# V in five blocks and tokens gathered from the output: one change to an attention kernel with routed experts

## The chip, the cores and the metric

The kernel runs on one core of a Trainium2 chip. The metric is device time in microseconds: the median of several executions of the whole program.

## The reference

There are two stages. The first is attention over 8 batches, 8 heads, 576 tokens and 64 channels. A query keeps only the keys whose score lies within `tau` of its best one:

```python
scores = q @ k.transpose(0, 1, 3, 2) / np.sqrt(64)
scores = np.where(scores >= scores.max(-1, keepdims=True) - tau, scores, -1e9)
attn = np.exp(scores - scores.max(-1, keepdims=True))
x = (attn / (attn.sum(-1, keepdims=True) + 1e-9)) @ v      # then laid out as 4608 tokens x 512
```

The second sends tokens through one of eight experts each. A token takes part if `x @ w_skip > 0`; the other tokens are the output as they stand:

```python
out = x.copy()
e_idx = np.argmax(xc @ w_gate, axis=1)                     # xc: the tokens that take part
out[token] = x[token] + gate_w[token] * (np.maximum(x[token] @ w1[e], 0) @ w2[e])
```

All is float32; the kernel keeps this accuracy by splitting each factor of a product into a high and a low part and adding three products.

## The kernel before

**Attention** is done head pair by head pair, 32 of them, four for each batch. For a pair `g`, `plan_pair` loads q and k (`raw`), ACT or DVE casts them to a high part and POOL or DVE subtracts to get the low part, both in a staging buffer `hl` (one of four buffers of the ring `wr`). `plan_dist` then spreads them by six transfers into the tile `QK`, and `plan_blk` by two into `BD` (the 64 last tokens of both heads). A staging buffer is free again when those transfers have read it. `plan_score` makes row maxima (PE, then DVE), `plan_thresh` and `plan_trow` turn them into a threshold row that ACT copies into QK (L848), `plan_weights` makes scores again, transposed, with the threshold subtracted (PE), `e` by an exponential (ACT, L884) and `p` by masking (DVE, L889). Two blocks of `p` share one of `PFB` buffers. From it come a half-precision high part (`phh`, ACT or DVE) and the rest (`phl`, POOL, L926); when POOL is done with it the buffer is free. `plan_av` multiplies both with V (PE, L954 to L958), and ACT copies the result out. POOL then normalises it: `fx` (L1006) into the batch's rows `xb`, `ft` (L1019) into `x2`, which holds the last 64 tokens of two batches.

A head has 576 = 4 x 128 + 64 keys. V is laid out on the host in `NT` = 6 blocks of 128 rows for each head: four full ones, one with the last 64 keys in rows 0 to 63, and one with the same keys in rows 64 to 127. The tail block of p holds the tail keys of the even head in its upper half and of the odd head in its lower half, so an even head uses block 4 and an odd one block 5. `plan_v` loads V of a batch in four transfers, finds a power of two to scale it (ACT, L623, with a sum of magnitudes), scales it (L686), casts it to half precision (L689) and subtracts (POOL, L692).

Finished rows of a batch are stored twice by `plan_rows` and `plan_tails`: to `xs`, a DRAM copy that tokens are gathered from, and to `out`. `plan_logits` and `plan_gate` compute the gate; records (token, weight) are scattered on POOL's queue into the list `lst` (L1312), sorted by expert.

**The order** of all this work on each engine isn't the program's. Every step is an `Op` with a duration for each engine that may do it, a key, and its predecessors; rings of buffers (`take`, `free`) add predecessors. `Plan.place` simulates the engines and a single DMA link with booked transfer times (`pl.dma(..., xfer)`), and puts the steps in the order in which they come free. `Plan.run` repeats this with priorities disturbed by each number in `SEEDS`, the last pass emitting the instructions. The order so found is fixed at build time, and each engine runs its own part in order.

**The experts** follow in program order. `plan_early` and the last part of the plan do layer 1 of a first job, 256 tokens of the fullest expert; then eight jobs follow. For each, `gather_x` turns the list's token numbers into indices and gathers rows into `xg` on POOL's queue. A list entry without a token holds 65536. `prep_x` transposes and splits, `layer1` and `layer2` multiply, `split_w` splits the weights (ACT, then DVE and POOL by turns, L1734), and `store` adds and scatters to `out`. Tokens beyond the planned capacity would be done by a loop at the end, whose blocks `late_table` finds in small operations on one partition, one after each block of layer 1.

Of the kernel before, what the change touches and what calls it, by code (L numbers as in the profile page):

```python
# [27 lines left out]
H = 8  # L28
# [25 lines left out]
NT = NM + 2  # L54
# [6 lines left out]
PFB = 3  # L61
# [233 lines left out]
def attn_moe_kernel(ctx: ExitStack, tc: tile.TileContext, qk, vl, tau, wg, w1, w2, out):  # L295
# [14 lines left out]
    xs = dp.tile([NTOK, DM], F32, name="xs")  # L310
# [78 lines left out]
    linit = cp.tile([P, NB, 2], F32, name="linit")  # L389
# [82 lines left out]
    def init():  # L472
# [17 lines left out]
    def plan_pair(g):  # L490
# [16 lines left out]
        ld = pl.dma(k - OFF["ld"], load, (ring.take("xb", 2) if g == 1 else ring.take("raw", 1)) + ([(T["neg"],)] if g else []), [1.8], 0.46)  # L507
# [40 lines left out]
    def plan_blk(g):  # L548
# [12 lines left out]
        T["bd", g] = pl.dma(k - OFF["bd"] if g else -200, blk, [*T["lo", g]] + ring.take("BD", 2), [0.41, 0.41], 0.66)  # L561
        T["hld", g] += [T["bd", g]]

    def plan_dist(g, h):
# [10 lines left out]
        for i in range(3):  # L575
# [11 lines left out]
            mine.append(pl.dma(kd + 0.1 * i, dist, [*c] + ([(mine[0],)] if mine else qr), [1.5], 0.65))  # L587
# [3 lines left out]
    def plan_v(b):  # L591
# [16 lines left out]
        for i in range(4):  # L608
# [5 lines left out]
                    [1.15],  # L614
# [245 lines left out]
    def plan_weights(g, i):  # L860
# [75 lines left out]
        elif i == STEP - 1:  # L936
            plan_av(g, 1, [(i - 2, [0, 1]), (NM, [NM + 1]), (i, [2, 3])], n)

    def plan_av(g, h, parts, n):
# [23 lines left out]
        for j, (i, kts) in enumerate(parts):  # L963
# [9 lines left out]
            if NM not in kts:  # L973
                ring.free("ph", [x]) if NM + 1 not in kts else ring.free("tp", [x])
# [364 lines left out]
    kk = cp.tile([P, 2, E, E], F32, name="kk")  # L1339
# [3 lines left out]
    idg = cp.tile([P, E, CT], I32, name="idg")  # L1343
    evs = {}

    class Job:
        def __init__(self, cap, rec, ids, idg):
            self.cap, self.rec, self.ids, self.idg = cap, rec, ids, idg
# [5 lines left out]
    j0 = Job(CAPE, rec0, id0[:, 0, :], id0[:, 1, :])  # L1354
    jobs = [j0] + [
        Job(CAPS[e] - (CAPE if e == 0 else 0), recs[:, e], ids[:, e], idg[:, e]) for e in range(E)
# [34 lines left out]
    def plan_early(k, j):  # L1391
# [24 lines left out]
        def ids():  # L1416
            nc.vector.tensor_copy(id0[:, 0, :], rec0[:, :, 0])
            nc.vector.tensor_scalar(id0[:, 1, :], rec0[:, :, 0], float(NTOK - S - 1), None, op0=ALU.min)
# [5 lines left out]
        for t in range(CAPE // P):  # L1424

            def ga(t=t):
                if t == 0:
                    early["xg"] = cp.tile([P, CAPE // P, DM], F32, name="xg0")
                gather(early["xg"][:, t, :], id0[:, 1, t : t + 1], NTOK - S)
# [232 lines left out]
    T["init"] = pl.dma(OFF["init"], init, [settle[1]], [0.1, 0.3, 1.2, 0.4])  # L1662
# [53 lines left out]
    tab = cp.tile([1, 2 * NOV + 1], I32, name="tab")  # L1716
    NK = E + 1
    rows = []
# [60 lines left out]
    def store(j, t, yp):  # L1779
# [11 lines left out]
        for x in rows:  # L1791
# [46 lines left out]
    def late_table():  # L1838
# [4 lines left out]
        ce = late.tile([1, 8, NK], F32, name="ce")  # L1843
        capv, capb, nbk, cum, prv, colb, eve, tmp = (ce[:, i, :] for i in range(8))
# [32 lines left out]
        yield  # L1877
        nc.vector.tensor_scalar(
# [21 lines left out]
        yield  # L1900
        lp_ = [1, NOV, NK]
# [12 lines left out]
        ej = late.tile([1, 2, NOV], F32, name="ej")  # L1914
        for i, src in enumerate((eve, colb)):
# [8 lines left out]
        nc.vector.tensor_copy(tab[:, 0 : 2 * NOV], ej.rearrange("p a j -> p (a j)"))  # L1924
# [6 lines left out]
    for part in parts:  # L1931
        part()
    w1s = early["w1"]
# [48 lines left out]
    with tc.For_i(0, nit, 1) as it:  # L1982
# [15 lines left out]
        nc.sync.dma_start(wb, w2v[ds(ev, 1)].rearrange("a p t f -> p (a t) f"))  # L1998
# [82 lines left out]
```

## Time and profile before

| what | value |
|---|---|
| median of 3 runs | 942.32 us (941.84 to 942.96) |
| profiled execution | 938.75 us |
| span of its trace, first to last instruction | 937.0 us |
| mean granted TensorE clock | 0.966 |
| busy share of the span | PE 93%, DVE 74%, ACT 67%, POOL 71% |
| transfers | 157.37 MB, mean 168 GB/s |

The trace is of one execution. "Busy" is the share of the time in which an engine executes; an engine waits in order for the inputs of its next instruction, and the trace names what ended the wait. The clock is the share of full speed that the chip granted to TensorE, which has two levels, 1.2 and 2.4 GHz. A DMA share of 1 means that all sixteen DMA engines move data all the time.

### The profile page before, as it was taken

How to read it: one execution, taken by the hardware profiler on the slowest of the kernel's cores; microseconds unless marked ns; L12 is line 12 of the kernel's file. 1: busy time of each engine (PE TensorE's matmuls, PEld its weight loads, DVE VectorE, ACT ScalarE, POOL GpSimd, SP SyncE). 2: the span in 40 equal slices, each digit the busy share in tenths (PEclk: the TensorE clock that was granted, in tenths of full speed). 3: DMA queues.
4: the chain of work that ended last, by engine and by line, in shares of the span. 5: the costliest groups of instructions: out<-in, count | busy, mean ns of one | idle time of the engine just before them, and what ended most of it. 6: DMA issues, size and time to landing. Idle time of an engine off the chain costs nothing. (4 is left out here: it accounts for less than half of the span.)

```text
span 937.0 us, 24810 instructions
## 1 busy us (share of the span) xinstructions
PE 870.6 (93%) x9630; PEld 808.6 (86%) x9630; DVE 691.5 (74%) x1622; ACT 628.7 (67%) x947; POOL 662.2 (71%) x452
## 2 busy tenths in 40 slices
PE   6899998998999999999998999978889999999994
PEld 3789997997999998899997898867879898999993
DVE  4888986888888888889895898967525554487770
ACT  1588986886998897899896699768414442455450
POOL 5288884896788898999987799968334545365451
PEclk8799998999999999999997999989989999999998
DMA  7987676669679759877866674623356535544530
GB/s 207 217 224 174 130 202 178 146 164 267 135 156 265 171 110 259 188 160 200 224 147 184 173 168 91 176 91 114 113 162 228 193 102 181 180 144 180 178 115 18
DMA packets 81790, 157.37 MB, mean 168 GB/s; under 512 B 28619, under 2 KB 28875, under 8 KB 81672
## 3 DMA queue, kind: packets, MB, share of 16 engines
q1 hardware_dynamic: 76984, 145.49, 59.4%
q0 software_dynamic: 4544, 10.28, 3.3%
q8 instruction: 77, 1.26, 0.5%
q14 instruction: 41, 0.34, 0.1%
q10 hardware_dynamic: 144, 0.00, 0.0%
HBM read 70.78 MB, written 24.78 MB: 102 GB/s over the span
## 5 line engine op out<-in xcount | busy, mean ns | idle before, releaser
L926 POOL TENSOR_TENSOR phl<-p,phh 128x1152 f16<-128x1152 f32 x128 | 305.4, 2394 | 58.5 <-ACT phh L465 16.1
L748 DVE TENSOR_REDUCE mx<-shp 128x1 f32<-128x288 f32 x558 | 236.7, 448 | 48.7 <-PE shp L743 45.5
L884 ACT ACTIVATE e<-sps,ntau 128x576 f32<-128x576 f32 x288 | 211.0, 740 | 57.4 <-PE sps L716 54.3
L889 DVE SCALAR_TENSOR_TENSOR p<-sps,e 128x576 f32<-128x576 f32 x288 | 215.4, 751 | 33.1 <-ACT e L884 24.9
L743 PE MATMUL shp<-QK 128*128 128x288 f32 x992 | 201.6, 314 | 6.1 <-DVE mx L748 3.2
L716 PE MATMUL sps<-QK 128*128 128x288 f32 x1024 | 191.7, 312 | 10.7 <-ACT QK L848 5.4
L716 PEld LDWEIGHTS sps<-QK 128*128 128x128 f32 x1024 | 148.7, 193 | 19.2 <-ACT QK L848 7.1
L743 PEld LDWEIGHTS shp<-QK 128*128 128x128 f32 x992 | 149.7, 191 | 12.8 <-DVE mx L748 7.8
L465 ACT ACTIVATE phh<-p 128x1152 f16<-128x1152 f32 x117 | 136.4, 1166 | 12.2 <-DVE p L889 8.1
L958 PE MATMUL avp<-Vh,phl 128*128 128x65 f16 x1280 | 130.8, 194 | 7.4 <-POOL phl L926 7.3
L954 PE MATMUL avp<-Vh,phh 128*128 128x65 f16 x1280 | 132.8, 196 | 2.6 <-ACT a L465 2.5
L957 PE MATMUL avp<-Vl,phh 128*128 128x64 f16 x1280 | 131.6, 193 | 0.0
L958 PEld LDWEIGHTS <-phl 128*128 128x128 f16 x1280 | 118.0, 98 | 8.2 <-POOL phl L926 8.1
L954 PEld LDWEIGHTS <-phh 128*128 128x128 f16 x1280 | 116.8, 98 | 8.1
L957 PEld LDWEIGHTS <-phh 128*128 128x128 f16 x1280 | 118.1, 99 | 3.0 <-issue 3.0
L1734 POOL TENSOR_TENSOR wl<-wr,wh 128x1024 fp32r<-128x1024 f32 x28 | 72.5, 2601 | 35.4 <-ACT wh L1733 30.0
L1771 PE MATMUL hps<-xh,wl 128*128 128x256 f32 (+4 forms) x256 | 77.1, 301 | 0.0
L1771 PE MATMUL hps<-xh,wh 128*128 128x256 f32 (+4 forms) x248 | 76.5, 308 | 0.1
L1771 PE MATMUL hps<-xl,wh 128*128 128x256 f32 (+4 forms) x248 | 75.0, 303 | 0.0
L1772 ACT ACTIVATE QK<-hps 128x256 fp32r<-128x256 f32 (+4 forms) x64 | 26.9, 421 | 68.9 <-PE hps L1771 68.2
L1783 POOL DMA_INDIRECT out<-o,ids x21 | 21.0, 1001 | 71.5 <-DVE o L1782 30.0
L692 POOL TENSOR_TENSOR Vl<-vraw,Vh 128x768 f16<-128x768 f32 x32 | 51.0, 1600 | 22.3 <-ACT Vh L689 22.1
(261 smaller groups left out, 1912.1 us busy)
## 6 DMA issues: line engine op xcount, KB each, us to landing
QK<-hl SPq DMA_DIRECT2D x192, 288.0 KB
wr<-in_w SPq DMA_DIRECT2D x31, 1024.0 KB
raw<-in_qk SPq DMA_DIRECT2D x32, 576.0 KB
vraw<-in_vl SPq DMA_DIRECT2D x32, 384.0 KB
xs<-xb SPq DMA_DIRECT2D x32, 256.0 KB
out<-xb SPq DMA_DIRECT2D x32, 256.0 KB
BD<-hl SPq DMA_DIRECT2D x64, 64.0 KB
xs<-x SPq DMA_DIRECT2D x8, 128.0 KB
```

Of the source, the lines that this page charges most:

```text
L465: nc.scalar.activation(dst, src, AF.Copy)
L716: nc.tensor.matmul(ps[:, j, 0:HS], w_, x_[:, js], start=(i == 0), stop=(i == len(mm) - 1))
L743: nc.tensor.matmul(ps[:, 0:HS], w_, x_[:, js], start=(q == 0), stop=(q == len(mm) - 1))
L748: nc.vector.tensor_reduce(T["mx", g][:, o, j : j + 1], T.pop(("S", g, i, j))[:, 0:HS], AX.X, ALU.max)
L884: nc.scalar.activation(e, T["W", g, i][:, :, 0:HS], AF.Exp, bias=ntau, scale=0.125)
L889: nc.vector.scalar_tensor_tensor(T[z][:, kt % 2].rearrange("p (a b) -> p a b", a=2), T.pop(("W", g, i))[:, :, 0:HS], 0.0, T.pop(("e", g, i ...
L926: nc.gpsimd.tensor_tensor(T["pl", g, i], T.pop(z)[:, 0:nk], T["ph", g, i], op=ALU.subtract)
L954: nc.tensor.matmul(pv[:, c, :], x, Vh[:, vh, kt, :], start=(j + q + c == 0), stop=False, skip_group_check=True)
L957: nc.tensor.matmul(pv[:, c, 0:D], x, Vl[:, vh, kt, :], start=False, stop=False, skip_group_check=True)
L958: nc.tensor.matmul(pv[:, c, :], y, Vh[:, vh, kt, :], start=False, stop=(c == NM), skip_group_check=True)
L1734: lo[q % 2].tensor_tensor(w[1][:, sl], rs, w[0][:, sl].bitcast(F32), op=ALU.subtract)
L1771: nc.tensor.matmul(hp_[:, 0:cap], w_, x, start=(i == 0), stop=(i == len(mm) - 1))
```

## The change

V loses its sixth block: block 4 holds the tail keys of even heads in its upper half and of odd heads in its lower half, and all heads use it. The copy `xs` goes, with its stores and an initialising write; gathers read `out`, and list entries without a token, whose numbers lie beyond the bound, are left out by the gather instead of being clipped, so the two `xg` buffers are zeroed once ahead. The gathers and scatters of different experts are declared independent. The late loop, which may no longer read a row that it has written, gets a count of valid entries. `linit` shares the memory of `kk`. There is a fourth p buffer, the planner's durations for most transfers are longer, and the order comes from other seeds.

```diff
-NT = NM + 2
+NT = NM + 1
-PFB = 3
+PFB = 4
...
 SEEDS = (
-    1000005, 1000007, 1000359, 1000371, ...
+    1000005, 1000007, 1000025, 1001369, ...
...
-    xs = dp.tile([NTOK, DM], F32, name="xs")
...
-            nc.vector.memset(vt[:, :, NM:, D : D + 1], 0.0)
-            nc.vector.memset(vt[0:TL, :, NM, D : D + 1], 1.0)
-            nc.vector.memset(vt[TL:P, :, NM + 1, D : D + 1], 1.0)
+            nc.vector.memset(vt[:, :, NM, D : D + 1], 0.0)
+            nc.vector.memset(vt[0:TL, 0::2, NM, D : D + 1], 1.0)
+            nc.vector.memset(vt[TL:P, 1::2, NM, D : D + 1], 1.0)
...
     def gather(dst, idx, n):
-        nc.gpsimd.indirect_dma_start(
+        return nc.gpsimd.indirect_dma_start(
             dst,
             None,
-            xs[0:n, :],
+            out[0:n, :],
...
-        nc.sync.dma_start(
-            xs[NTOK - S - TL : NTOK - S, :].rearrange("p (o c) -> p o c", c=P),
-            ident[0:TL].rearrange("p (o c) -> p o c", o=1).broadcast_to([TL, DM // P, P]),
-        )
...
-        ld = pl.dma(k - OFF["ld"], load, ..., [1.8], 0.46)
+        ld = pl.dma(k - OFF["ld"], load, ..., [2.0], 0.46)
-        T["bd", g] = pl.dma(..., [0.41, 0.41], 0.66)
+        T["bd", g] = pl.dma(..., [0.46, 0.46], 0.66)
-            mine.append(pl.dma(kd + 0.1 * i, dist, ..., [1.5], 0.65))
+            mine.append(pl.dma(kd + 0.1 * i, dist, ..., [1.6], 0.65))
-                    [1.15],
+                    [1.1],
...
-            plan_av(g, 1, [(i - 2, [0, 1]), (NM, [NM + 1]), (i, [2, 3])], n)
+            plan_av(g, 1, [(i - 2, [0, 1]), (NM, [NM]), (i, [2, 3])], n)
...
         for t in range(NM):
-            for i, dst in enumerate((xs, out)):
-
-                def st(t=t, dst=dst):
-                    r0 = b * S + t * P
-                    nc.sync.dma_start(dst[r0 : r0 + P, :], T["x", b][:, t, :])
-
-                rd.append(pl.dma(k + OFF["row"] + OFF["rsp"] * (2 * t + i), st, T["xm", b, HP - 1], [0.69], 0.7))
+            def st(t=t):
+                r0 = b * S + t * P
+                nc.sync.dma_start(out[r0 : r0 + P, :], T["x", b][:, t, :])
+
+            rd.append(pl.dma(k + OFF["row"] + OFF["rsp"] * 2 * t, st, T["xm", b, HP - 1], [0.75], 0.7))
...
-                for dst in (xs, out):
-                    nc.sync.dma_start(dst[r0 : r0 + TL, :], T["x2"][i * TL : (i + 1) * TL, :])
-        s = pl.dma(k + 1, st, xtm, [0.4] * 4)
+                nc.sync.dma_start(out[r0 : r0 + TL, :], T["x2"][i * TL : (i + 1) * TL, :])
+        s = pl.dma(k + 1, st, xtm, [0.45] * 2)
...
     def gather_x(j):
         nc.vector.tensor_copy(j.ids[:, 0 : j.nb], j.rec[:, 0 : j.nb, 0])
-        nc.vector.tensor_scalar(j.idg[:, 0 : j.nb], j.rec[:, 0 : j.nb, 0], float(NTOK - 1), None, op0=ALU.min)
-        j.xg = mp.tile([P, CT, DM], F32, name="xg", tag="xg")
+        j.xg = xgs.pop(0) if xgs else mp.tile([P, CT, DM], F32, name="xg", tag="xg")
         for t in range(j.nb):
             m = j.m(t)
-            gather(j.xg[0:m, t, :], j.idg[0:m, t : t + 1], NTOK)
+            gt = gather(j.xg[0:m, t, :], j.ids[0:m, t : t + 1], NTOK)
+            for x in rows:
+                tc.declare_no_dep(gt.ins, x.ins, reason="it uses no row of another expert")
+            reads.append(gt)
...
-        for x in rows:
+        for x in rows + reads:
             tc.declare_no_dep(sc.ins, x.ins, reason="every token goes to one expert")
...
+        nc.vector.tensor_copy(capv[:, E:NK], nbk[:, E:NK])
+        nc.vector.tensor_tensor(fin, prv, capb, op=ALU.subtract)
+        nc.vector.scalar_tensor_tensor(fin, fin, float(P), capv, op0=ALU.mult, op1=ALU.add)
-        for i, src in enumerate((eve, colb)):
+        for i, src in enumerate((eve, colb, fin)):
...
+        nc.vector.tensor_tensor(done, ej[:, 2, :], thr, op=ALU.subtract)
...
+    xgs = [mp.tile([P, CT, DM], F32, name="xg", tag="xg") for _ in range(2)]
+    for x in xgs:
+        nc.vector.memset(x, 0.0)
     w1s = early["w1"]
     gather_x(jobs[1])
...
+        dn = lp.tile([1, 1], F32, name="dn")
+        nc.sync.dma_start(dn, done[0:1, ds(it, 1)])
+        nc.tensor.matmul(dp_[:, 0:1], onesr, dn, start=True, stop=True)
+        nc.vector.tensor_scalar(dm, dp_[:, 0:1], iop, SENT, op0=ALU.is_gt, op1=ALU.mult)
+        nc.vector.tensor_tensor(li[:, 0:1], rc[:, 0:1], dm, op=ALU.add)
...
-    vl = np.zeros((B, P, H, NM + 2, D), np.float32)
+    vl = np.zeros((B, P, H, NM + 1, D), np.float32)
-    vl[:, 0:TL, :, NM] = vt
-    vl[:, TL:, :, NM + 1] = vt
+    vl[:, 0:TL, 0::2, NM] = vt[:, :, 0::2]
+    vl[:, TL:, 1::2, NM] = vt[:, :, 1::2]
```

## Rows read from the trace of the kernel before

**Rows 1.** Stretches: PE, PEld, DVE, ACT, POOL busy (instructions); clock, DMA share, GB/s.

```profile
40.00:640.00 600.00, 567.81 (x7583) 535.89 (x7582) 507.47 (x1292) 496.45 (x734) 502.36 (x310) 0.98 0.71 175
...
700.00:900.00 200.00, 198.03 (x1264) 184.10 (x1263) 123.05 (x174) 86.66 (x143) 105.20 (x62) 1.00 0.52 176
...
128.00:136.00 8.00, 7.90 (x118) 7.54 (x116) 7.00 (x14) 7.18 (x11) 6.88 (x5) 1.00 1.01 281
...
140.00:160.00 20.00, 16.26 (x167) 15.44 (x165) 12.82 (x27) 12.21 (x18) 7.53 (x6) 0.83 0.79 208
500.00:520.00 20.00, 15.49 (x98) 14.85 (x96) 8.90 (x24) 8.08 (x13) 10.58 (x9) 0.66 0.70 196
10.00:40.00 30.00, 21.14 (x91) 15.34 (x89) 16.54 (x53) 10.91 (x16) 7.89 (x35) 0.72 1.05 240
```

**Rows 2.** The instructions of line 842, one for each head pair.

```profile
L842 PE MATMUL sps<-ident,nh x32: 270/272/276, 37.8 to 629.6; 128*2 128x128 f32 x32
```

**Rows 3.** Waits of PE, 40 to 640 us: total, times, longest.

```profile
PE avp L958 <- POOL phl L926: 7.3, 5, 5.3
PE sps L716 <- ACT QK L848: 5.4, 4, 3.7
PE gps L1062 <- POOL x L1019: 3.6, 1, 3.6
...
PE avp L954 <- ACT a L465: 2.2, 3, 1.1
```

**Rows 4.** Timeline of SyncE's DMA issues, 128 to 140 us: start, length.

```profile
129.71 3.07 SPq L1125 DMA_DIRECT2D out<-xb  x3
132.83 2.95 SPq L1125 DMA_DIRECT2D xs<-xb  x3
...
139.38 2.30 SPq L581 DMA_DIRECT2D QK<-hl  x1
```

**Rows 5.** Timeline, 138 to 153 us; in brackets the idle time before.

```profile
143.16 1.16 ACT L465 ACTIVATE hl<-raw 128x1152 fp32r<-128x1152 f32 x1 [6.29 <-DMA QK<-hl]
...
145.44 0.81 PE L716 MATMUL sps<-QK 128*128 128x288 f32 x4 [3.74 <-ACT QK L848]
```

**Rows 6.** Timeline, 498 to 514 us, POOL.

```profile
505.35 0.39 POOL L1019 TENSOR_TENSOR x<-a,z 64x128 f32<-64x128 f32 x1 [3.63 <-DMA lst<-rec,si]
```

**Rows 7.** Timeline, 617 to 640 us, DVE.

```profile
623.80 0.76 DVE L889 SCALAR_TENSOR_TENSOR p<-sps,e 128x576 f32<-128x576 f32 x1 [3.85 <-POOL phl L926]
```

**Rows 8.** DMA issues: count, size of one, or us to landing.

```profile
vraw<-in_vl SPq DMA_DIRECT2D x32, 384.0 KB
xs<-xb SPq DMA_DIRECT2D x32, 256.0 KB
...
lst<-rec,si POOLq DMA_INDIRECT x36, 3.9
```

**Rows 9.** Groups by line and shape: busy us, mean ns, idle before.

```profile
L692 POOL TENSOR_TENSOR Vl<-vraw,Vh 128x768 f16<-128x768 f32 x32 | 51.0, 1600 | 22.3 <-ACT Vh L689 22.1
...
L686 ACT ACTIVATE vraw<-vraw,vmx 128x768 f32<-128x768 f32 x32 | 29.6, 939 | 0.0
...
L689 ACT ACTIVATE Vh<-vraw 128x768 f16<-128x768 f32 x32 | 26.9, 854 | 0.0
...
L623 ACT ACTIVATE Vh<-vraw 128x1536 f16<-128x1536 f32 x16 | 23.7, 1484 | 16.5 <-DMA vraw<-in_vl 16.5
```

**Rows 10.** The same view of DVE in the first 20 us.

```profile
L359 DVE MEMSET QK<- 64x1152 f32 x2 | 2.0, 1018 | 0.4 <-issue 0.4
```

**Rows 11.** Timelines of POOL, DVE and PE, 640 to 715 us.

```profile
676.77 1.94 POOL L1312 DMA_INDIRECT lst<-rec,si  x1 [0.30 <-DVE wl L1734]
679.01 0.97 POOL L1312 DMA_INDIRECT lst<-rec,si  x1 [0.30 <-issue]
...
684.13 0.17 DVE L1739 CAST ids<-recs 128x2 int32<-128x2 f32 x1 [5.13 <-DMA recs<-lst]
...
688.54 0.33 PE L1753 MATMUL xtp<-ident,xg 128*128 128x128 f32 x1 [2.22 <-DMA xg<-xs,idg]
```

More of the change, by code (lines that the diff above doesn't have):

```diff
@@ L82 @@
 SEEDS = (
[5 rows of a table removed]
+    1000005, 1000007, 1000025, 1001369, 1001397, 1001554, 1001677, 1001694, 1001761, 1001833, 1002643, 1002698,
+    1002871, 1003002, 1003249, 1003775, 1003868, 1006562,
 )
@@ L505, in gate_q @@
             nc.vector.tensor_scalar(q, q, tpos, None, op0=ALU.mult)
-        ld = pl.dma(k - OFF["ld"], load, (ring.take("xb", 2) if g == 1 else ring.take("raw", 1)) + ([(T["neg"],)] if g else []), [1.8], 0.46)
+        ld = pl.dma(k - OFF["ld"], load, (ring.take("xb", 2) if g == 1 else ring.take("raw", 1)) + ([(T["neg"],)] if g else []), [2.0], 0.46)
         x = ld if g else pl.op(k - OFF["hl"], gate_q, [ld], {DVE: 0.37})
@@ L559, in blk @@
                 )
-        T["bd", g] = pl.dma(k - OFF["bd"] if g else -200, blk, [*T["lo", g]] + ring.take("BD", 2), [0.41, 0.41], 0.66)
+        T["bd", g] = pl.dma(k - OFF["bd"] if g else -200, blk, [*T["lo", g]] + ring.take("BD", 2), [0.46, 0.46], 0.66)
         T["hld", g] += [T["bd", g]]
@@ L585, in dist @@
                     nc.sync.dma_start(dst[D:P, RQ2 : RK3 + 1], src[:, HQH : HKL + 1 : 3])
-            mine.append(pl.dma(kd + 0.1 * i, dist, [*c] + ([(mine[0],)] if mine else qr), [1.5], 0.65))
+            mine.append(pl.dma(kd + 0.1 * i, dist, [*c] + ([(mine[0],)] if mine else qr), [1.6], 0.65))
         T["qk", g, h] = mine
@@ L973, in plan_av @@
             if NM not in kts:
-                ring.free("ph", [x]) if NM + 1 not in kts else ring.free("tp", [x])
+                ring.free("ph", [x])
+            elif h:
+                ring.free("tp", [x])
         def cpy(e):
@@ L1338, in attn_moe_kernel @@
     tabp = cp.tile([1, E], I32, name="tabp")
-    kk = cp.tile([P, 2, E, E], F32, name="kk")
     k0, oh = kk[:, 0], kk[:, 1]
@@ L1342, in attn_moe_kernel, with __init__ @@
     ids = cp.tile([P, E, CT], I32, name="ids")
-    idg = cp.tile([P, E, CT], I32, name="idg")
     evs = {}
     class Job:
-        def __init__(self, cap, rec, ids, idg):
-            self.cap, self.rec, self.ids, self.idg = cap, rec, ids, idg
+        def __init__(self, cap, rec, ids):
+            self.cap, self.rec, self.ids = cap, rec, ids
             self.nb = -(-cap // P)
@@ L1352, in m @@
             return min(P, self.cap - t * P)
-    j0 = Job(CAPE, rec0, id0[:, 0, :], id0[:, 1, :])
+    j0 = Job(CAPE, rec0, id0[:, 0, :])
     jobs = [j0] + [
-        Job(CAPS[e] - (CAPE if e == 0 else 0), recs[:, e], ids[:, e], idg[:, e]) for e in range(E)
+        Job(CAPS[e] - (CAPE if e == 0 else 0), recs[:, e], ids[:, e]) for e in range(E)
     ]
@@ L1417, in ids @@
             nc.vector.tensor_copy(id0[:, 0, :], rec0[:, :, 0])
-            nc.vector.tensor_scalar(id0[:, 1, :], rec0[:, :, 0], float(NTOK - S - 1), None, op0=ALU.min)
+            nc.vector.tensor_scalar(id0[:, 1, :], rec0[:, :, 0], float(NTOK - S - TL - 1), None, op0=ALU.min)
         o = pl.op(k + 1, ids, [o], {DVE: 0.15})
@@ L1428, in ga @@
                     early["xg"] = cp.tile([P, CAPE // P, DM], F32, name="xg0")
-                gather(early["xg"][:, t, :], id0[:, 1, t : t + 1], NTOK - S)
+                gather(early["xg"][:, t, :], id0[:, 1, t : t + 1], NTOK - S - TL)
             gs.append(pl.op(k + 2, ga, [o, *stored] + [(y,) for y in gs[-1:]], {POOL: 1.04}, lat=3.0, port=()))
@@ L1661, in attn_moe_kernel @@
     T["settle"] = settle
-    T["init"] = pl.dma(OFF["init"], init, [settle[1]], [0.1, 0.3, 1.2, 0.4])
+    T["init"] = pl.dma(OFF["init"], init, [settle[1]], [0.1, 0.3, 1.2])
     T["start"][1] = [(T["qk", 0, 1][-1],)]
@@ L1716, in attn_moe_kernel @@
     tab = cp.tile([1, 2 * NOV + 1], I32, name="tab")
+    done = cp.tile([1, NOV], F32, name="done")
     NK = E + 1
-    rows = []
+    rows, reads = [], []
     def split_w(src, raws=(), lo=(nc.vector, nc.gpsimd)):
@@ L1842, in late_table @@
         yield
-        ce = late.tile([1, 8, NK], F32, name="ce")
-        capv, capb, nbk, cum, prv, colb, eve, tmp = (ce[:, i, :] for i in range(8))
+        ce = late.tile([1, 9, NK], F32, name="ce")
+        capv, capb, nbk, cum, prv, colb, eve, tmp, fin = (ce[:, i, :] for i in range(9))
         kc = kk[r0, 0]
@@ L1877, in late_table @@
         yield
+        nc.vector.tensor_copy(capv[:, E:NK], nbk[:, E:NK])
+        yield
         nc.vector.tensor_scalar(
@@ L1900, in late_table @@
         yield
+        nc.vector.tensor_tensor(fin, prv, capb, op=ALU.subtract)
+        yield
+        nc.vector.scalar_tensor_tensor(fin, fin, float(P), capv, op0=ALU.mult, op1=ALU.add)
+        yield
         lp_ = [1, NOV, NK]
@@ L1913, in late_table @@
         yield
-        ej = late.tile([1, 2, NOV], F32, name="ej")
-        for i, src in enumerate((eve, colb)):
+        ej = late.tile([1, 3, NOV], F32, name="ej")
+        for i, src in enumerate((eve, colb, fin)):
             nc.vector.tensor_tensor(cm[:, 1], cm[:, 0], rowb(src), op=ALU.mult)
@@ L1923, in late_table @@
         yield
-        nc.vector.tensor_copy(tab[:, 0 : 2 * NOV], ej.rearrange("p a j -> p (a j)"))
+        nc.vector.tensor_tensor(done, ej[:, 2, :], thr, op=ALU.subtract)
+        yield
+        nc.vector.tensor_copy(tab[:, 0 : 2 * NOV], ej[:, 0:2].rearrange("p a j -> p (a j)"))
         yield
@@ L2003, in attn_moe_kernel @@
         nc.gpsimd.indirect_dma_start(
-            xo, None, xs[:, :], bass.IndirectOffsetOnAxis(ap=li[:, 1:2], axis=0), bounds_check=NTOK - 1, oob_is_err=False
+            xo, None, out[:, :], bass.IndirectOffsetOnAxis(ap=li[:, 1:2], axis=0), bounds_check=NTOK - 1, oob_is_err=False
         )
@@ L2055, in layout @@
         "in_qk": qk,
-        "in_vl": vl.reshape(B, P, H * (NM + 2) * D),
+        "in_vl": vl.reshape(B, P, H * (NM + 1) * D),
         "in_tau": np.asarray(tau, np.float32).reshape(1),
```

6 lines of the change are left out of this document (4 added, 2 removed), and 5 rows, old and new, of the table SEEDS.

## The prediction

> **What bounds the kernel now.** I read the stretches first. From 40 to 640 us the kernel does attention: TensorE (PE) is busy 567.81 of 600 us, VectorE (DVE), ScalarE (ACT) and GpSimd (POOL) 507, 496 and 502 each [rows 1]. From 700 to 900 us it does the experts, with PE busy 198.03 of 200. So the experts give back 2 us at most, and nearly all that this change can move is the 32.2 us that PE idles in attention, and what the lower level of its clock costs there: the clock is 0.98 on the mean, 2% of 600, some 12 us. Nothing else fills 900 us as closely, so I price every edit by what it does to PE's waits.
>
> A head pair passes every (629.6 - 37.8) / 31 = 19.1 us [rows 2]. The waits of PE in attention [rows 3] show who ends them: the low half of p by POOL 7.3 us, of which one wait alone is 5.3; the threshold copy by ACT 5.4, one alone 3.7; a normalised tail by POOL 3.6, a single wait; the copy of an attention result by ACT 2.2. The idle time is thus partly three large stalls (5.3, 3.7 and 3.6, 12.6 of 32.2 us) and partly crumbs.
>
> Stall A, at 140 us. SyncE issues three row stores to `out` from 129.71 and three to `xs` from 132.83 and, behind them, the loads that spread a pair into QK, the last at 139.38 [rows 4]. In 128 to 136 us the DMA engines are full (share 1.01, 281 GB/s) [rows 1]. ACT's cast of the next pair needs its staging buffer back from those spreading transfers and waits 6.29 us for them; ACT takes its work in order, so the threshold copies behind it are late, and PE waits 3.74 us at 145.44 [rows 5]. After it PE runs at 0.83 of its clock through 140 to 160 us, a third of that time at the lower level (1.2 GHz): 20 x 0.17 = 3.4 us. The stall costs about 7.1 us.
>
> Stall B, at 505 us. POOL's product x (L1019) waits 3.63 us until the list scatters issued just before it have landed, and PE's transpose of it waits as long [rows 3, 6]. In 500 to 520 us the clock is 0.66 [rows 1], so 20 x 0.34 = 6.8 us more are lost: 10.4 us.
>
> Stall C, at 620 us, is POOL late with a low half (the 5.3 us of [rows 3]); meanwhile DVE's next p waits 3.85 us, because all three p buffers wait for POOL [rows 7].
>
> **The change, part by part.** *No second copy.* Of 64 row stores of 256 KB the 32 to `xs` go [rows 8], with half of the sixteen tail stores and one initialising store. For one batch that is 4 x 0.262 = 1.05 MB; at the 281 GB/s of the full stretch, 3.7 us of transfer in front of the spreading loads. ACT's wait of 6.29 becomes 2.6, and PE's 3.74 next to nothing: 3.7 saved. What is late next is ACT's own backlog, which DVE's and PE's queued work covers. With a gap that short the clock may hold; I take half of its 3.4 us. Together 5.4 us; from below 0 (the new order can put other transfers there), from above the whole 7.1. At the other batch ends I take nothing: PE's table of waits names no other one of size that a transfer ends. SyncE issues 41 stores fewer; it is on no wait of PE.
>
> The gathers read `out` instead of `xs`: equal rows, equal size, and the same stores have to land before them. Scatters to `out` of other experts are declared independent, so no wait is added.
>
> *V in five blocks.* V loads shrink from 384 KB by a sixth [rows 8]; the ACT passes over V from 1536 and 768 elements to 1280 and 640, POOL's from 768 to 640 [rows 9]. From 1484 and 854 ns an element of ACT costs (1484 - 854) / 768 = 0.82 ns: 16 x 256 x 0.82 = 3.4 us for the first pass and 32 x 128 x 0.82 = 3.4 us for each of the other two, 10.1 us in all; in plain proportion it is (16 x 1484 + 32 x (939 + 854)) / 6 = 13.5. POOL saves up to 32 x 1600 / 6 = 8.5 us beside it. Neither engine sets the pace by itself. Outside the three stalls, PE's large waits on ACT and POOL are 2.0 + 1.7 + 2.2 = 5.9 of its 32.2 us idle [rows 3], 18%, so I count 18% of 10.1, 1.9 us. The rest is covered by PE's and DVE's own work. The ends are 0 and 13.5. PE's products with V stay equal in number and size, since each head used only one of the two tail blocks.
>
> At the start, 10 to 40 us, the DMA engines are full too (1.05, 240 GB/s) [rows 1], and 0.26 MB of V less is 1.1 us; part of V comes behind the first spreading loads, so I take 0.6. The ends are 0 and 1.1.
>
> *Fourth p buffer.* Nothing in it makes POOL faster. In stall C PE itself waits for POOL, so the 3.85 us of DVE are mostly hidden behind that; a free buffer lets DVE have its next p done (0.8 us or so) when POOL returns. I take 1.0, with 0 and 3.85 as ends.
>
> *Order and bookings.* The bookings move no instruction by themselves; they shape the planner's order. The trace of before doesn't show the new order. Its bounds: the best order removes all that is left of PE's idle time and clock loss in attention, 32.2 + 12 - 8.3 = 36 us; each further stall of B's kind costs 10.4 us. Nearest to a value is that the average order stays as it is, so 0; I keep one B either way, +10.4 and -10.4, for the range, and two on the slow side.
>
> *Experts.* Two memsets of 128x1536 stand on DVE ahead of the first expert's index copy. By the memset of 1152 elements in 1018 ns [rows 10], 1.36 us each, 2.7 together; DVE idles 5.13 us just there, waiting for the records [rows 11], which hides them. If that cover went, the gather and PE's first transposes (which already wait 2.22 us) would be 2.7 us later. They can fall on the last list scatters of POOL: a scatter beside DVE's weight split took 1.94 us, one beside nothing 0.97 [rows 11]. If memsets did the same to two scatters, the chain scatter, records, gather would be 1.9 us longer; I take 0, since a memset reads nothing from SBUF and that split reads two operands. The Trainium skill (SBUF — State Buffer, Who interferes with whom) says that a VectorE instruction with at most one SBUF input, outside the two-port modes, does not contend with GpSimd; by that the cost is 0, by the row up to 1.9, and the trace of before has no memset beside a scatter to tell. Six more one-partition operations on DVE for the late table, and eight index operations fewer, lie under PE's 198.03 of 200 us [rows 1]: 0, with 2 as the upper end. The loop of late blocks grows, but no gather of its own runs here, by the list of DMA issues.
>
> The sum is 5.4 + 1.9 + 0.6 + 1.0 = 8.9 us. The profiled execution took 938.75 us (span 937.0 and 1.75 around it), which gives 929.9; the median shown is 942.32, 3.57 above it, and so 933.4 for the median.
>
> **Rivals.**
> 1. *The order also loses B.* For it: DMA and POOL have more room, and B hangs on where a scatter stands before x. Against it: the planner books a scatter on POOL but knows nothing of this wait. 933.4 - 10.4 = 923.0.
> 2. *More waits of B's kind; the other side.* 36 scatters and 32 products x share POOL's queue in the new order. POOL waited for such a landing at 505 us with PE in step. One further stall brings 943.8 and eats the gain; from the second on the kernel is slower: 954.2, less if PE's clock holds (about 948). What decides is whether x stands within some 4 us behind a scatter, with PE's transpose next.
> 3. *The saved transfers were hidden, and the change does nothing for PE.* Then ACT's 6.29 us at A would come back in another place, since its in-order queue meets the staging buffer anyway: 942. For it: only one wait of PE in attention goes back to transfers. Against it: the direct chain at A.
> 4. *The memsets hold the chain*, 2.7 + 1.9 us: 938.0. Against it: 5.13 us of cover.
> 5. *The gathers wait for the scatters after all.* Then the change of source would add a landing, but an expert's rows are needed a whole layer later, and PE's 198 of 200 us would stay: inside the forecast.
>
> **How the numbers follow.** A measurement of this kernel tells about 0.2%, 1.9 us, from no change. Forecast (about 926 to 940): 0.42. Rival 1: 0.22. Rival 4: 0.04. Rival 3, or one stall more: 0.10. Rival 2 with two stalls: 0.22. Faster is 0.42 + 0.22 + 0.04 = 0.68, same 0.10, slower 0.22. The time is the forecast's, 933.4. For eight in ten the range leaves out the far ends of rivals 1 and 2: from 915, half of the way that the order could still go, to 951, between one and two more stalls.
>
> **What would show it.** Right: no `xs` rows; full DMA stretches shorter at the batch ends; no wait of ACT's cast for QK transfers over 3 us; ACT's passes over V near 1.27 and 0.75 to 0.83 us, POOL's near 1.33; PE idle in attention near 25 us; the experts' 200 us unchanged. Wrong: PE's waits on x or on low halves with more than one of over 3 us each, and a clock below 0.98 in attention; a first gather later behind its records; or full transfers at other places, with ACT waiting there.

## The result and the profile after

The changed kernel takes 927.0 us (median of 4 runs, 924.5 to 928.4) beside 942.1 for the kernel before on the same chip (4 runs): a ratio of 0.985, 95% interval 0.980 to 0.990. It is faster by 15 us; 933.4 was predicted, with a gain of 8.9. The profiled execution took 926.21 us (span 924.4). Two runs of the experiments below, 1049 us of a_tail_dve and 1284 us of s2_own_tile, fell into a slower state of the chip (granted clock 0.74 and 0.59) and are left out of every ratio and median.

The same stretches as in [rows 1], of the kernel after, and one more:

```profile
40.00:640.00 600.00, 568.79 (x7673) 538.27 (x7674) 502.60 (x1281) 502.22 (x747) 507.35 (x318) 0.98 0.63 160
700.00:900.00 200.00, 198.52 (x1281) 184.95 (x1280) 124.30 (x181) 87.27 (x147) 104.56 (x62) 1.00 0.49 165
128.00:136.00 8.00, 8.00 (x106) 7.72 (x106) 6.82 (x18) 6.88 (x10) 6.77 (x5) 1.00 0.95 244
140.00:160.00 20.00, 19.93 (x265) 19.08 (x264) 17.55 (x45) 17.28 (x26) 15.00 (x11) 1.00 0.77 186
500.00:520.00 20.00, 18.48 (x231) 17.78 (x230) 14.10 (x46) 12.39 (x19) 15.29 (x11) 0.86 0.55 162
10.00:40.00 30.00, 21.53 (x103) 16.66 (x101) 16.62 (x53) 12.64 (x20) 11.70 (x38) 0.77 1.06 242
580.00:600.00 20.00, 14.82 (x154) 13.57 (x152) 13.13 (x49) 8.69 (x11) 13.89 (x11) 0.83 0.45 109
```

In 140 to 160 us PE is busy 19.93 of 20 us at full clock, where it was 16.26 at 0.83: stall A is gone. The experts' stretch is as before. But PE's busy time in 40 to 640 us has hardly grown (568.8 for 567.8), since 23 us behind the last pair now lie inside that stretch instead of 10, and since 580 to 600 us shows a new hole. From the first pair to the last PE idles 26.5 us, 29.6 before. The waits of PE in 40 to 640 us, for [rows 3] (total, times, longest), say which stalls are left:

```profile
PE shp L736 <- DVE mx L741: 5.5, 14, 0.9
PE sps L709 <- DVE p L882: 4.3, 11, 0.8
PE gps L1057 <- POOL x L1014: 3.6, 1, 3.6
PE avp L951 <- POOL tpl L919: 3.0, 1, 3.0
PE sps L709 <- ACT QK L841: 2.4, 4, 1.2
```

Stall B stands as it was: GpSimd's product x waits for a scatter, and PE waits 3.6 us for x, at 498 us instead of 505 [rows 3, 6]. Stall C is smaller: PE waits 3.0 us, not 5.3, for a low half, at 630 us. That low half stands behind a product x again, the same one as at 618 us before, which now waits for a gather (timelines of GpSimd and PE):

```profile
498.18 0.39 POOL L1014 TENSOR_TENSOR x<-a,z 64x128 f32<-64x128 f32 x1 [4.23 <-DMA lst<-rec,si]
...
624.69 1.23 POOL L451 DMA_INDIRECT xg<-out,id  x1 [0.97 <-DVE id L1409]
628.52 0.39 POOL L1014 TENSOR_TENSOR x<-a,z 64x128 f32<-64x128 f32 x1 [2.60 <-DMA xg<-out,id]
...
630.32 0.23 PE L951 MATMUL avp<-Vh,tpl 128*128 128x65 f16 x1 [3.05 <-POOL tpl L919]
```

Neither is the hole at 580 us. The passes over V have shrunk as worked out [rows 9]:

```profile
L685 POOL TENSOR_TENSOR Vl<-vraw,Vh 128x640 f16<-128x640 f32 x32 | 43.6, 1368 | 3.5 <-ACT Vh L682 3.1 <-ACT e L877 0.2
L679 ACT ACTIVATE vraw<-vraw,vmx 128x640 f32<-128x640 f32 x32 | 25.8, 831 | 0.0
L682 ACT ACTIVATE Vh<-vraw 128x640 f16<-128x640 f32 x32 | 23.3, 744 | 0.0
L616 ACT ACTIVATE Vh<-vraw 128x1280 f16<-128x1280 f32 x16 | 20.3, 1270 | 11.0 <-DMA vraw<-in_vl 11.0
```

yet ACT is busier in 40 to 640 us than before (502.2 for 496.5) and GpSimd too (507.4 for 502.4): the planner gave them work that VectorE did, of the high parts of q and k 27 casts of 32 to ACT (20 before), of the low parts 43 subtractions of 64 to GpSimd (34 before).

The clearest ruler is the row of line 842 [rows 2], one instruction per head pair. Before it runs from 37.8 to 629.6 us (591.8), after from 33.1 to 616.8 (583.7). In these two traces the start gave 4.7, attention 8.1, all behind the last pair nothing (307.4 and 307.6 us to the end of the span). The start's 4.7 were lost again by the sixth pair (threshold copies at 120.0 us before, 121.1 after).

### The profile page after: what moved, and what is told of

It is laid out like the page before. It is cut to its first block, busy times and chain, and to the rows that moved or that the text cites. A ratio compares the mean times of both kernels' runs of the same rounds, so it can differ in the third digit from the quotient of the medians.

```text
span 924.4 us, 24769 instructions
## 1 busy us (share of the span) xinstructions
PE 863.4 (93%) x9630; PEld 804.1 (87%) x9630; DVE 682.4 (74%) x1604; ACT 629.2 (68%) x956; POOL 664.0 (72%) x461
## 5 line engine op out<-in xcount | busy, mean ns | idle before, releaser
L736 PE MATMUL shp<-QK 128*128 128x288 f32 x992 | 198.4, 312 | 9.9 <-DVE mx L741 5.3
L462 ACT ACTIVATE phh<-p 128x1152 f16<-128x1152 f32 x121 | 140.9, 1164 | 17.8 <-DVE p L882 11.2
L515 POOL TENSOR_TENSOR hl<-raw,hl 128x576 fp32r<-128x576 f32 x43 | 61.6, 1440 | 20.9 <-ACT hl L462 17.5
```

The costliest lines, as they stand in the source:

```text
L462: nc.scalar.activation(dst, src, AF.Copy)
L736: nc.tensor.matmul(ps[:, 0:HS], w_, x_[:, js], start=(q == 0), stop=(q == len(mm) - 1))
```

## Experiments

All ratios are to the kernel before on the same chip, measured in turn with it, so that they can be set side by side. The last column is the stretch from the first to the last row of [rows 2] in the one profiled run. "Old order" is the order and the bookings of the kernel before, instruction for instruction as its planner gave them; only what is issued differs.

| kernel | order | ratio, 95% interval | pairs, us |
|---|---|---|---|
| before | old | 1 | 37.8 to 629.6: 591.8 |
| after | new | 0.985 [0.980, 0.990] | 33.1 to 616.8: 583.7 |
| s1_no_copy | old | 0.986 [0.982, 0.990] | 37.0 to 614.7: 577.7 |
| s2_plus_five | old | 0.985 [0.980, 0.989] | 35.6 to 612.2: 576.6 |
| s3_plus_p4 | old | 0.986 [0.981, 0.990] | 38.0 to 616.2: 578.2 |
| a_xs_back | new | 0.988 [0.983, 0.992] | 32.4 to 613.4: 581.0 |
| s1_xs_unread | old | 0.992 [0.989, 0.996] | 36.1 to 620.6: 584.5 |
| s1_xs_few | old | 0.987 [0.982, 0.992] | 37.5 to 619.1: 581.6 |
| s2_tail_dve | old | 0.991 [0.987, 0.994] | 35.9 to 622.6: 586.7 |
| a_tail_dve | new | 0.995 [0.993, 0.997] | 34.2 to 624.6: 590.4 |
| s2_own_tile | old | 0.971 [0.967, 0.975] | 38.6 to 609.8: 571.2 |
| a_hold_scatters | new | 0.983 [0.978, 0.988] | 32.9 to 611.5: 578.6 |
| a_own_p3 | new | 0.987 [0.983, 0.992] | 33.6 to 619.4: 585.8 |
| b_five_own | old | 0.985 [0.981, 0.990] | 36.2 to 616.1: 579.9 |

### One part after the other, in the old order

s1 issues no store to the second copy and gathers from `out`; its part with the experts is that of the changed kernel:

```diff
-            for i, dst in enumerate((xs, out)):
+            for i, dst in enumerate((None, out)):
                 def st(t=t, dst=dst):
+                    if dst is None:
+                        return
...
-            xs[0:n, :],
+            out[0:n, :],
```

> The order of the kernel before, instruction for instruction, and its bookings, V and p buffers; only the second copy goes: no store to xs is issued (the stores to out stay where they were), the gathers read out, and the experts' part is that of the changed kernel. Theory (the prediction's term): the wait of ACT's cast at 143 us goes from 6.29 to some 2.6 us, PE's 3.74 us at 145 us nearly vanishes, and the kernel gains 5.4 us on the 942.1 of before: 936.7, bounds 935.0 to 942.1; the table of PE's waits else as before, stalls B and C in place. Rival 1: the transfers were hidden and the gain is the new order's: 942. Rival 2: every batch end gains, not only the one at 130 us: 933 or less.

Measured 0.986: 13 us (9 to 17) under before, the whole gain of the change from this part alone. Stall A is gone; the same stretches as above of s1:

```profile
128.00:136.00 8.00, 7.91 (x120) 7.49 (x120) 6.52 (x13) 7.14 (x11) 6.88 (x5) 1.00 0.92 247
140.00:160.00 20.00, 19.86 (x262) 18.76 (x261) 18.79 (x44) 17.50 (x28) 13.58 (x8) 1.00 0.79 220
```

and of its PE waits in 40 to 640 us the first ones:

```profile
PE avp L954 <- POOL phl L922: 7.3, 5, 5.3
PE gps L1058 <- POOL x L1015: 3.6, 1, 3.6
PE sps L712 <- DVE p L885: 3.5, 12, 0.4
```

B (3.6) and C (5.3) stand unchanged to a tenth, and the 3.7 us behind ACT's threshold copy have shrunk to 1.0 (two such waits, 1.2 together); ACT's cast waits 1.9 us for transfers there, 2.6 in the forecast. From the sixth to the eighth pair the kernel before takes 43.8 us (copies at 120.0 and 163.8), s1 36.7: 7.1 us less, the upper bound of the forecast. From there to the last pair it is 467.2 and 460.1, another 7.1 us, in pieces of 0.6 to 2.1 us near the batch ends, of which the forecast had none. Rival 2 of the expectation was right. At three of these places (from the 10th, the 15th and the 18th row of line 842 to the next, 3.2 us together) ACT waits in the kernel before for V loads, which SyncE issues among and behind the row stores. The waits of ACT for these loads in 40 to 640 us, in before and in s1_xs_unread (below, with the stores put back); s1 has none:

```profile
ACT Vh L623 <- DMA vraw<-in_vl: 5.5, 4, 2.2
ACT Vh L620 <- DMA vraw<-in_vl: 1.7, 2, 1.4
```

s2 adds the five blocks, s3 the fourth p buffer (`bufs=PFB + 1` in the tile, 3 in the plan).

> As s1, and V in five blocks per head (loads, passes of ACT and POOL), still in the order of before. Theory: 1.9 us less than s1 in attention and 0.6 at the start, so 2.5 us under s1 (bounds 0 to 14.6): about 934.2 if s1 gives 936.7; PE's waits on ACT and POOL outside the three stalls shorter. Rival: PE waits for these engines only in the stalls, so shorter passes change nothing: within 1 us of s1.

> As s2, and a fourth p buffer, still in the order of before. Theory: DVE's wait of 3.85 us for a p buffer at 623 us goes, worth 1.0 us (bounds 0 to 3.85): about 933.2 if s2 gives 934.2. Rival: POOL is the late one there, so PE's wait on the low half (5.3 us) stays and the time is that of s2. What is left between this kernel and the changed one (927.0) is then the new order with its bookings: theory 0 plus or minus one stall (10.4); if the three steps give what they should, the order gave 6 us.

s2 came out 1.1 us under s1 by the ratios and 1.1 by the pairs, inside the interval; s3 gave nothing. VectorE's wait of 3.8 us for a p buffer, still there in s2, is gone in s3, but PE still has 7.1 us in four waits for a low half, one of 5.3, as the rival said: where GpSimd is the late one, a buffer more for its input doesn't help PE. From s3 to the changed kernel, which has the same parts, nothing is left for the new order: 0.986 and 0.985. In the two profiles it starts 4.9 us earlier and then takes 5.5 us longer over the pairs (583.7 for 578.2).

### Is it the traffic?

Three kernels put the stores to the second copy back, to a buffer that nothing reads: a_xs_back in the changed kernel, s1_xs_unread in s1, and s1_xs_few in s1 with 8 of 512 columns:

```diff
-                nc.sync.dma_start(out[r0 : r0 + P, :], T["x", b][:, t, :])
+                for dst in (xs, out):
+                    nc.sync.dma_start(dst[r0 : r0 + P, :], T["x", b][:, t, :])
...
+                    if dst is xs:
+                        nc.sync.dma_start(dst[r0 : r0 + P, 0:8], T["x", b][:, t, 0:8])
```

> The changed kernel in its own order, with the second copy's stores put back: each row store and each tail store is issued twice, the first to a buffer that nothing reads. Theory: the traffic alone costs what its removal gave, 5.4 us (0 to 7.1): 932.4, with ACT's cast waiting for the QK transfers again at a batch end. Rival 1: the new order has room for the stores at the batch ends, so the traffic is hidden: 927. Rival 2: an order made without these stores meets them in more places than one: 937 or more.

> As s1 (order and bookings of the kernel before, gathers from out), with all row and tail stores to the second copy issued again at their old places, to a buffer that nothing reads. Theory (it is the traffic): stall A is back, ACT's cast waits some 6 us for QK transfers at 143 us, and the 12.2 us that s1 gained go: 935 to 938 beside a before of 937. Rival (it is the reading: gathers, their dependences and the experts' index work): the time stays that of s1, 925.

> As s1_xs_unread, but each store to the second copy takes only the first 8 of its 512 columns: as many stores on SyncE's queue, as long a hold on the buffer of rows, 1/64 of the bytes. Theory (bytes ahead of the QK loads): the time of s1, 925, within 2 us. Rival (the queue's slots and the buffer held longer): most of the loss comes back, 932 or more.

In the old order the stores as such, their slots on SyncE's queue and the longer hold on the row buffer, cost nothing (0.987 for 0.986). Their bytes cost 0.6%, 6 us (0.992; the two kernels, on one chip, take 934.3 us in the median of 12 runs and 928.1 in that of 4). That lies between theory and rival, and isn't all of the 13: s1_xs_unread is still 7 us (4 to 10) under before. What then differs is the source of the gathers with what belongs to it (index operations, declared independences, two memsets, the late table) and one initialising store, and nothing behind the last pair is shorter for them: from the last row of [rows 2] to the end of the span it is 307.4 us in before, 307.8 in s1. That half stays open. The one profiled run of s1_xs_unread doesn't help: at 926.6 us it was the fastest of its 12 (median 934.3), and in it PE waits at most 1.3 us at stall A's place. In that run the stores take back 1.6, 2.4 and 2.9 us of what s1 had gained, from the 7th, the 10th and the 18th row of line 842 to the next, and nothing of note elsewhere.

In the new order the same traffic costs 0.3%, inside the interval, as rival 1 had it: ACT waits 5.1 us for V loads again and PE 1.9 us for a threshold copy at 139.8 us, but 140 to 160 us stays at full clock with PE busy 19.92. So "the second copy costs 13 us" holds for one order of the row stores and the loads, not for the traffic by itself.

### What stands behind stalls B and C

In the traces of before and after, the products x that wait for list scatters, or for a gather, all belong to odd batches: 64 partitions that start at partition 64. Those of the even batches start at 0 and don't wait for one, even straight behind it (GpSimd, after):

```profile
219.14 1.17 POOL L1305 DMA_INDIRECT lst<-rec,si  x1 [0.18 <-issue]
220.34 0.41 POOL L1014 TENSOR_TENSOR x<-a,z 64x128 f32<-64x128 f32 x1
```

No value that x reads or writes is a scatter's. Two ways of taking the wait away were tried; the first runs the odd ones on VectorE:

```diff
-            nc.gpsimd.tensor_tensor(
+            (nc.vector if b % 2 else nc.gpsimd).tensor_tensor(
                 T["x2"].rearrange("p (h d) -> p h d", d=D)[rs, 2 * hp : 2 * hp + 2],
...
-        if not seen:
+        if not seen or o.fn.__name__ == "ft" and o.fn.odd:
             return
```

The last lines take these products out of an ordering that the kernel keeps otherwise: GpSimd's next instruction waits for VectorE's last one before it.

> As s2 (order of before, no copy, V in five blocks), and the tail products x of the odd batches (64 partitions by 128, 16 of the 32) run on VectorE at the same place of the order; GpSimd keeps those of the even batches. In every trace so far only such a product of an odd batch waits for list scatters to land. Theory: stall B (PE 3.8 us at 489 us and 10.2 us at half clock, so 5.1) and most of stall C (GpSimd idles 4.0 us at 596 to 600 us for the same reason, PE waits 5.3 at 606 and runs 6.8 us at half clock, so 3.4) go: 9 to 14 us, 909 to 914. Rival 1: B alone goes, C is set by the three scatters behind it: 914 to 915. Rival 2: the wait moves to the next product on GpSimd, or VectorE's 16 extra instructions (some 0.3 us each) take it back: 921 or more.

> The changed kernel with the same edit: odd batches' tail products on VectorE. Theory: its stall B (PE 3.6 us at 498 us and 6.8 us at half clock, so 3.4) goes, 7 us: 920; the stall at 580 us (six scatters in a row) stays. Rival 1: 924 or more, the waits of PE go to others. Rival 2: the order of the changed kernel has a further wait of this kind at 624 us that matters too: 916.

Both missed: 0.991 against 0.985 (rival 2), and 0.995 against 0.985 (rival 1). Stalls B and C did shrink (2.2 and 5.9 us less from one pair to the next there than in s2), but more was lost on the way. No x on VectorE waits for a scatter, though it writes the same rows of the same tile (one starts 0.2 us behind a scatter's start, at 611.92 us), so the wait isn't one for the tile's contents. What was lost shows in the timelines of VectorE and GpSimd in s2_tail_dve (start, length):

```profile
314.56 2.00 DVE L1018 TENSOR_TENSOR x<-a,z 64x128 f32<-64x128 f32 x1
...
314.03 2.38 POOL L923 TENSOR_TENSOR phl<-p,phh 128x1152 f16<-128x1152 f32 x1 [0.79 <-DVE phh L467]
```

and in all sixteen (min, median, max in ns):

```profile
L1018 DVE TENSOR_TENSOR x<-a,z x16: 289/813/3007, 141.4 to 656.6; 64x128 f32<-64x128 f32 x16
```

x takes 0.29 us at the least and here stands still while a low half runs on GpSimd: it ended at 316.56, GpSimd's operation at 316.41. The Trainium skill (SBUF — State Buffer, SBUF: two separate sides) says that a VectorE operation with two SBUF inputs and a GpSimd operation that reads SBUF take a shared pair of ports as an exclusive lock, whole instruction by whole instruction; the trace agrees. These products with the ordering kept weren't tried.

The second way leaves x on GpSimd and gives the odd batches a tile of their own, written over all 128 partitions (the lower half of it is never used):

```diff
-            rs = slice(r0, r0 + TL)
+            if hp == 0 and b % 2:
+                T["x3"] = ap_.tile([P, DM], F32, name="x3", tag="x3", bufs=1)
+            rs = slice(0, P) if b % 2 else slice(0, TL)
...
-                T["x2"].rearrange("p (h d) -> p h d", d=D)[rs, 2 * hp : 2 * hp + 2],
+                T["x3" if b % 2 else "x2"].rearrange("p (h d) -> p h d", d=D)[rs, 2 * hp : 2 * hp + 2],
...
+                if key[0] == "t":
+                    nc.tensor.transpose(ps[:, t, :], T["x3"][:, t * P : (t + 1) * P], ident)
+                    nc.tensor.transpose(ps[:, t, 0:TL], T["x2"][0:TL, t * P : (t + 1) * P], ident[0:TL, 0:TL])
+                    continue
```

> As s2 (order of before, no copy, V in five blocks; 0.985 of before), and the tail products x of the odd batches stay on GpSimd but go to a tile of their own over all 128 partitions, so that none of them starts at partition 64; PE transposes the two tiles into one bank (8 small transposes for 4, four times in the kernel). In s2_tail_dve the stalls at 489 and 606 us went as expected (2 and 6 us come back there), but x on VectorE took up to 3.0 us instead of 0.29 while GpSimd was at work, and cost more. Theory: without that contention the wait for list scatters goes and nothing takes its place: 7 to 12 us under s2, 0.972 to 0.978 of before. Rival 1: only stall B goes (PE 3.8 us, half clock 10.2 us): some 5 us under s2, 0.980. Rival 2: GpSimd's wait is not what PE waits for; the scatters behind it are: 0.985.

It took 914.3 us (median of 6) beside 940.9: 0.971, by the ratios 13 us under s2, a little more than expected, and 13 under the changed kernel, and the fastest version here (the profiled run, 919.5 us, was its slowest). GpSimd's timeline at stall B's place:

```profile
492.06 1.07 POOL L1318 DMA_INDIRECT lst<-rec,si  x1 [0.30 <-issue]
493.13 0.43 POOL L1020 TENSOR_TENSOR x<-a,z 128x128 f32<-128x128 f32 x1
493.48 2.40 POOL L923 TENSOR_TENSOR phl<-p,phh 128x1152 f16<-128x1152 f32 x1
```

x runs straight behind a scatter. At stall C's place s2 has x 3.98 us late, with the low half that PE wants behind it and two more scatters:

```profile
594.87 1.00 POOL L1312 DMA_INDIRECT lst<-rec,si  x1 [0.93 <-DVE tab L1379]
599.85 0.39 POOL L1018 TENSOR_TENSOR x<-a,z 64x128 f32<-64x128 f32 x1 [3.98 <-DVE mx L745]
600.57 1.34 POOL L1312 DMA_INDIRECT lst<-rec,si  x1 [0.33 <-POOL x L1018]
602.22 0.97 POOL L1312 DMA_INDIRECT lst<-rec,si  x1 [0.30 <-issue]
603.25 2.36 POOL L923 TENSOR_TENSOR phl<-p,phh 128x1152 f16<-128x1152 f32 x1
```

So C was the same wait as B, seen one instruction later; the view names VectorE as what came last, but x starts 4.98 us behind the start of a scatter, as at stall B (4.75 us in before), the order of the work didn't change between the two kernels, and x lost its 4 us. The wait is thus tied to where x is written. The edit changes the tile, the starting partition and the number of partitions together; a tile of its own that starts at 64 wasn't tried, and why such an instruction waits, no run shows. In 40 to 640 us s2_own_tile has PE busy 582.64 us at 0.99, and no wait of PE is longer than 1.2 us.

b_five_own puts the same tile into the kernel before, second copy and all (V in five blocks, to make room):

> The kernel before in its order, with the second copy and the gathers from it, V in five blocks (for the room), and the tile of its own for the odd batches' tail products. Theory: without any of the change's saved stores, stalls B (3.6 us and 13.7 us at half clock: 10.4) and C (5.3 and 6.8 at half clock: 8.7) go, less the 2 us by which five blocks gave anything: 12 to 19 us in the profile, 8 to 14 in the median as in s2_own_tile: 0.985 to 0.991 of before. Rival: stall A and the copy's traffic hold the later batches, so the gain is under 4 us: 0.996.

0.985, as expected: without one saved store it gains what the changed kernel gains, and stall A stays (PE busy 15.96 us at 0.83 in 140 to 160 us). a_own_p3 puts it into the changed kernel, with three p buffers for the room:

> The changed kernel in its own order, with three p buffers again (the fourth's room is needed) and the odd batches' tail products in a tile of their own over 128 partitions, as in s2_own_tile. The two kernels then have the same parts in two orders. Theory: stall B of the changed kernel goes (PE 3.6 us, 6.8 us at half clock: 7 us), the stall at 580 us stays, and the third buffer costs nothing: 0.977 of before, 6 us over s2_own_tile, which is what the new order costs. Rival 1: the new order was made for four p buffers and VectorE now waits for GpSimd: 0.985 or more. Rival 2: the orders are equally good once this wait is gone: 0.971.

0.987: no gain, rival 1. B is gone (2.1 us less from the 26th to the 27th pair than in the changed kernel) and the wait of 3.0 us at 630 us is down to 0.4, but 4.9 us were lost up to the 26th pair: VectorE's p waits 2.4 us in two waits for GpSimd, which the changed kernel hasn't, and PE waits 4.9 us for p up to 490 us where the changed kernel waits 2.7. The new order was made for four buffers; the old one runs as well on three. That the third buffer is the reason is argued from these waits: three buffers alone in the new order weren't tried, nor B's worth there with four (the room is missing).

### The new stall at 580 us

In the changed kernel six list scatters in a row (576.75 to 584.15 us) keep GpSimd from the low halves, and PE is busy 14.82 us in 580 to 600 us, at 0.83 of its clock. a_hold_scatters issues the nine of that pair of batches one behind each low half:

```diff
...
+        if o.fn.__name__ == "fpl" and self.held:
+            self.put(self.held.pop(0))
...
```

> The changed kernel, with the nine list scatters of the third pair of batches held back and issued one behind each following low half of p, in place of six in a row at 577 to 584 us (with 3.9 us of waiting for their indices before them). Theory: GpSimd's 11 us block at 573 to 584 us goes, and with it PE's wait for a low half (3.0 us), its gaps of about 1.1 us and 6.8 us at half clock (3.4): 6 to 8 us under the changed kernel, 0.977 of before. Rival: the last batches' gate and gathers then come later and take it back: 0.985.

0.983 against 0.985: a miss of the size, within the interval of no gain. Several things were wrong with it. The wait of 3.0 us for a low half isn't here but at 630 us. In the hole itself PE waits once for an operation of the gate and else for nothing that the profile shows ("issue"):

```profile
581.31 0.42 PE L736 MATMUL shp<-QK 128*128 128x288 f32 x2 [1.22 <-DVE rs L1213]
582.73 0.29 PE L736 MATMUL shp<-QK 128*128 128x288 f32 x1 [1.00 <-issue]
584.15 0.35 PE L736 MATMUL shp<-QK 128*128 128x288 f32 x1 [1.13 <-issue]
```

And a_xs_back has the same six scatters in a row (578.32 to 585.71 us) without the hole: PE is busy 17.52 us in 580 to 600 us there, at full clock. So the scatters alone don't make it, and its cause stays open. GpSimd had idled 0.45 us before those scatters, not 3.9 (that was its queue's wait, beside running work). And the low half that moved up met another wait:

```profile
572.38 0.39 POOL L1027 TENSOR_TENSOR x<-a,z 64x128 f32<-64x128 f32 x1
578.26 2.39 POOL L932 TENSOR_TENSOR phl<-p,phh 128x1152 f16<-128x1152 f32 x1 [5.49 <-DVE ca L1231]
580.81 1.01 POOL L1318 DMA_INDIRECT lst<-rec,si  x1 [0.15 <-PE shp L749]
```

That is the kernel's ordering of GpSimd behind VectorE; with the scatters out of the way it fell on the gate's operations. In the profiled run the pairs took 5.1 us less than in the changed kernel, and all behind the last pair 3.3 us more (310.9 for 307.6), as the rival has it.

## Why the prediction was right, and where not

Sign and range held, the time was 6 us too high. The terms, one by one:

- **No second copy**, priced at 5.4: with the gathers that belong to it, it gave 13 (9 to 17) in the order for which it was worked out. Stall A gave its whole upper bound of 7.1, since the clock held fully and not by half. The step that failed is "at the other batch ends I take nothing", read from PE's table of waits: 7.1 us more came off after the eighth pair. For 3.2 of them the traces show a way: ACT waited for V loads issued among and behind the row stores, and PE's table names only the last link there (p, a, a threshold copy). ACT's wait for these loads stood in [rows 9], 16.5 us in all (5.5 of it in 40 to 640 us), and wasn't priced. For the other 4 us no transfer was found, and since the stores put back cost 6 of the 13, how much of the rest is traffic stays open.
- **V in five blocks**, 1.9 and 0.6 at the start: some 1 us by s2, not to be told from nothing. The passes took what was worked out (1.27 for 1.27; 0.74 and 0.83 inside 0.75 to 0.83 but for a hundredth; 1.37 for 1.33).
- **Fourth p buffer**, 1.0: nothing in the old order, though the wait that it was to take went. In the new one it seems to be needed (a_own_p3).
- **Order and bookings**, 0: right in sum. But in the profiles it was two things, 4.9 us won at the start and 5.5 lost over the pairs, with a smaller stall C and the new hole at 580 us. PE's idle time in 40 to 640 us, forecast near 25 us, is 31.2.
- **Experts**, 0: 307.4 and 307.6 us behind the last pair. The two memsets took 1.34 us each (1.36 in the forecast), and the scatters beside them the 0.97 of an undisturbed one (VectorE and GpSimd, 669 to 675 us, after):

```profile
669.64 1.34 DVE L1937 MEMSET xg<- 128x1536 f32 x1 [0.27 <-issue]
671.25 1.34 DVE L1937 MEMSET xg<- 128x1536 f32 x1 [0.27 <-issue]
674.42 0.17 DVE L1731 CAST ids<-recs 128x2 int32<-128x2 f32 x1 [1.83 <-DMA recs<-lst]
...
669.39 0.97 POOL L1305 DMA_INDIRECT lst<-rec,si  x1 [0.30 <-issue]
670.67 0.97 POOL L1305 DMA_INDIRECT lst<-rec,si  x1 [0.30 <-issue]
```

  So rival 4 fell; of the cover's 5.13 us [rows 11] 1.83 are left.
- **Rival 1** didn't happen: B stayed. **Rival 2** didn't come either: there are two waits of B's kind, as before (3.6 and 3.0 us for 3.6 and 5.3), and what was taken as a sign of being wrong, more than one such wait of over 3 us, was there from the start. Its "about 948" doesn't follow from its figures: two stalls of 3.6 us at full clock give 940.6. **Rival 3** is refuted by s1 for the old order, and holds for the new one, where the same stores cost nothing that can be told.
- **What can be told**: the forecast took 1.9 us as the least difference that shows; the interval of the result is some 4.3 us to either side, and 24 runs of the kernel before on one chip lie between 936.7 and 948.0 us.
- **B and C**: each was read as a stall of its own, C as "POOL late with a low half". They are one cause. A tile of its own for x is worth 13 us in the old order, and with the second copy as much, five blocks included: as much as the change.

That the time came near is in part luck: the main term gave more than twice its price, and the parts named beside it gave less than they were priced at.

## What to carry to other kernels

Price traffic by the queue that it delays, at every place where it recurs, and don't let a table of one engine's waits stand for the cost of a transfer: its first victim can be an engine whose lateness reaches that engine under another name. Where one part of a change can be issued alone in an unchanged order, do it first; here it carried all of the gain in that order, and the other parts nothing that could be told. And where an instruction waits for something that it doesn't use, look for what sets it apart from its sisters that don't wait (here the tile and the partition at which it starts); moving it to another engine can cost more than the wait.

## What the runs showed of the hardware

- A product x of two SBUF operands (64x128) took 289 ns on VectorE at the least and beside GpSimd's work up to 3007 ns in s2_tail_dve (at 502.73 us, beside a scatter's issue and a low half) and 3612 ns in a_tail_dve.
- A list scatter's issue occupies GpSimd for 0.99 us in the median of 36 (0.97 to 1.94, after), but an instruction made to wait for it starts 4.7 to 5.4 us after the issue began (492.94 and 498.18 us, after).
- Stores of 32 bytes a partition in place of 2 KB, in the same number, cost the kernel nothing outside the interval (s1_xs_few, 0.987 for 0.986).
- The start varies from run to run of nearly the same program: the first row of [rows 2] lies between 35.6 and 38.6 us in the old order, with the same instructions ahead of it but for the loads of V. So does the end: from the last of these rows to the end of the span it is 304.2 us (s1_xs_unread) to 310.9 (a_hold_scatters). Part of every difference of 1 to 3 us between single profiles is that.
